# One Trainium2 core, sparse attention into a softplus MLP: weight loads gated by real waits, grouped reads of PSUM banks, query copies on GpSimd

## The chip, the cores and the metric

The kernel runs on one core of one Trainium2 chip. The metric is device time in microseconds (us). Engines are called PE (TensorE, matmuls), PEld (its weight loads), DVE (VectorE), ACT (ScalarE), POOL (GpSimd) and SP (SyncE, which here only issues DMAs). A change of under about 1% cannot be told from none.

## The reference

Inputs are fp32: q, k and v of 4 batches x 8 heads x 768 positions x 64, w_in of 512 x 2048 and w_out of 2048 x 512. The keys are cut into 24 chunks of 32. For each query an upper bound of its product with each chunk is taken from the chunk's smallest and largest key values; only the 6 best causal chunks are attended.

```python
k_min = np.min(k_chunks, axis=3);  k_max = np.max(k_chunks, axis=3)
ub = sum(maximum(q * k_min, q * k_max), axis=-1)        # per query and chunk, causal only
top_chunks = np.argsort(ub, axis=-1)[..., -top_k:]       # top_k = 6
scores = where(chosen chunk and causal, q @ k.T / sqrt(64), -1e9)
x = (softmax(scores) @ v)  laid out as (3072 tokens, 512)
h = x @ w_in;  g = maximum(h, 0) + log1p(exp(-abs(h)));  out = g @ w_out
```

## The kernel before

The work is cut into 12 blocks of 256 query rows (4 batches x 3 blocks). A block n has these steps, named as the code names its tasks: loads of k, q and v (`ld`), transposes of k and q, chunk minima and maxima `kx` from the transposed keys, copies `ka` and `kb` of the keys (head 0 and head 1 of a pair), the positive and negative part of the queries `qp` and `qn`, the bound matmuls `ub`, top-6 selection (`uba`, `max`, `lt`), a mask that is transposed (`mT`) and put into the query tiles as extra contraction rows (`ma`, `mb`), the second query tile `qa`, then per head pair p the score matmuls `s` with `exp` on ACT (`ex`), the diagonal mask on POOL (`cm`), `av`, normalisation (`rc`, `nm`), and the transposed result x (`oT`, `xe`). The MLP of a block is 16 tasks `h` (4 matmuls of 256 columns each), `exp` and `ln(1+.)` on ACT, and 16 tasks `y` (2 matmuls of 512 columns each). The first three blocks, the ramp, are loaded as fp32 and transposed by PE (L398, L459); from block 3 on POOL casts to bf16 (`ck`, `cq`, `cv`; L365, L367) and SP issues DMA transposes (L419, L469, L559, L659).

The order on each engine is set by a planner in the kernel: every task has a duration, a priority and its dependencies, and a discrete-event loop (`Graph.schedule`) lays the tasks out; they are then emitted in that order. Nothing else keeps the order: each engine works through its own list, and waits only for semaphores that the data or a reused buffer need. All loads of blocks go through the SP queue (a few through ACT's), the two weight loads through POOL's queue, in four pieces each (L326, L334). Where two engines read one PSUM bank, the second waits for the first.

In the planner `gates` makes block 2's loads follow the third piece of w_in, and `LGATE` makes the loads of block 3 and later follow the third piece of w_out. These are dependencies of the plan alone: the instructions have no wait for them.

Of the kernel before, what the change touches and what calls it, by code (L numbers as in the profile page):

```python
# [20 lines left out]
NP = H // 2  # L21
QB = 256
# [11 lines left out]
LEAD = 30  # L34
DMA_START = 1.3
MSTART = 20.0
AHEAD = 1.16
ORDER = ("0", "1", "wi", "2", "wo")
# [16 lines left out]
class Graph:  # L55
# [34 lines left out]
    def schedule(self):  # L90
# [58 lines left out]
        while True:  # L149
# [24 lines left out]
            for e in LAT:  # L174
# [14 lines left out]
                for b in t.bufs:  # L189
                    if b.slot is None:  # L190
# [16 lines left out]
def build(nc, tiles):  # L207
# [67 lines left out]
    for i in range(2):  # L275
        add("DVE", 0.3, lambda i=i: DV.memset(T("bd", i), 0.0), -9 + i * 30, w=[("bd", i)], name="bd0")
        add("DVE", 1.1, lambda i=i: DV.memset(T("mr", i), 0.0), -8 + i * 12, w=[("mr0", i)], name="mr0")
        add("DVE", 0.1, lambda i=i: DV.memset(T("v", i)[:, :, :, D:D + 1], 1.0), -8 + i * 30,
            w=[("v1", i)], name="v1")
        add("DVE", 1.35, lambda i=i: DV.memset(T("kb", i)[0:32], 0.0), -7 + i * 30, w=[("kb0", i)], name="kb0")  # L280

        def oh(which, i, blk):
            ks = slice(blk * QB, (blk + 1) * QB)
            dst = T("ka", i)[64:96, :, ks] if which == "ka" else T("kb", i)[32:64, :, ks]
            PO.tensor_copy(dst, T("ohb")[:, ks].unsqueeze(1).to_broadcast([32, NP, QB]))
        for blk in range(NBLK):
            for which in ("ka", "kb"):
                add("POOL", 0.95, lambda which=which, i=i, blk=blk: oh(which, i, blk), -6 + i * 34 + blk * 5, r=["ohb"],
                    w=[(which + "c", i, blk)], name="oh" + which)
# [49 lines left out]
    def gates(n):  # L339
        return [landed["wi", 2]] if n == 2 else []  # L340

    ramp_loads(0, -100)
    ramp_loads(1, -90)
    w_in_load(-50, [landed[1, "q", 1]])
    ramp_loads(2, -80)
    w_out_load(-40, [landed[2, "q", 1]])
    LGATE = [landed["wo", 2]]
# [26 lines left out]
    def prep(n):  # L374
# [12 lines left out]
        if ramp:  # L387
            for hh in range(2):
# [19 lines left out]
                for m in range(2):  # L408
                    add("DVE", 0.6, lambda m=m, red=red: red(m), pr + 0.1, r=[kT], w=[(kx, m, hh)], name=f"kx{n}")
                add("ACT", 0.48, lambda kab=kab: kab("ka", slice(0, 64)), pr + 0.2, r=[kT],  # L410
                    w=[("ka", i, j, hh) for j in js], name=f"ka{n}")
                add("ACT", 0.48, lambda kab=kab: kab("kb", slice(64, 128)), pr + 0.2, r=[kT],
                    w=[("kb", i, j, hh) for j in js], name=f"kb{n}")
# [59 lines left out]
        for hs in ([[0], [1]] if ramp else [[0, 1]]):  # L473
# [7 lines left out]
            add("DVE", 0.09 + 0.13 * len(hs), lambda sl=sl: DV.tensor_copy(T(qa)[0:64, sl], T(qb)[0:64, sl]), pr + 2,  # L481
                r=[(qb, hh, z) for hh in hs for z in range(3)], w=[(qa, hh, 0) for hh in hs], name=f"qa{n}")
        bds = [("bdw", i, h, k_) for h in range(2) for k_ in range(blk + 1)]
        ubp = ps("o")
        ns = len(sel)
        halves = [[0], [1]]
        for hs in halves:
# [15 lines left out]
            def uba(es=es, ne=ne):  # L503
# [239 lines left out]
def kernel(  # L743
# [30 lines left out]
    one("ohb", "ohb", [32, S], BF16)  # L774
    one("cmask", "cmask", [128, NQT, NCH], F32)
# [44 lines left out]
```

## Time and profile before

| what | value |
|---|---|
| median of 3 runs | 281.82 us (281.0 to 283.47) |
| the profiled execution's own time | 280.93 us |
| its span, first to last instruction | 279.2 us |
| busy PE / ACT / DVE / POOL | 248.9 / 198.6 / 152.5 / 98.3 us |
| HBM read / written | 27.26 / 6.29 MB |
| chain that ended last, by engine | PE 62%, DVE 16%, DMA 13%, ACT 4% |

PE is busy for 89% of the span, and the idle rest is not spread evenly: most of it lies in the first 53 us. Busy shares are means over stages, so the stages have to be read one by one. Times of rows are from the span's start.

### The profile page before, as it was taken

To read this page: it belongs to the slowest core of one execution; us is meant where nothing else is said; L and a number is where in the kernel's file an instruction comes from. 1 tells how busy PE (TensorE), PEld (TensorE's weight loads), DVE (VectorE), ACT (ScalarE), POOL (GpSimd) and SP (SyncE) were. 2 spreads that over 40 slices of the span, in tenths; PEclk is the share of its full clock that TensorE was granted. 3 is DMA by queue.
4 is the path that set the end of the run, shared out by engine and by line. 5 is a ranking of instruction groups with operands and counts; after the bars stand their busy time and mean duration, and the time that the engine had idled before them with its cause. 6 is when DMAs were issued, how large, how long until landed. Compare 5 with 4: busy or idle time off the path is not lost.

```text
span 279.2 us, 6479 instructions
## 1 busy us (share of the span) xinstructions
PE 248.9 (89%) x2424; PEld 184.4 (66%) x2460; DVE 152.5 (55%) x558; ACT 198.6 (71%) x355; POOL 98.3 (35%) x188
## 2 busy tenths in 40 slices
PE   3356796999999899989899988999999999999994
PEld 2244584777767668767676855866767777677661
DVE  6787837823979978479669536536326211020001
ACT  2436278898649876999796975686958969949470
POOL 8958327036318453438344432021311201100000
PEclk9999589999999999999999999999999999999999
DMA  8999979949999999999999993412312211040101
GB/s 165 218 182 164 197 135 184 189 80 134 241 231 191 258 220 198 248 187 173 248 218 222 215 230 82 113 41 59 94 39 73 44 39 40 1 77 38 40 38 75
DMA packets 120800, 39.23 MB, mean 140 GB/s; under 512 B 113600, under 2 KB 117696, under 8 KB 120768
## 3 DMA queue, kind: packets, MB, share of 16 engines
q1 hardware_dynamic: 113392, 33.83, 62.7%
q0 software_dynamic: 4224, 4.19, 9.3%
q10 hardware_dynamic: 3152, 0.79, 1.6%
q8 instruction: 19, 0.31, 0.5%
q14 instruction: 13, 0.11, 0.1%
HBM read 27.26 MB, written 6.29 MB: 120 GB/s over the span
## 4 chain that ended last, share of the span: by engine, by line
PE 62%; DVE 16%; DMA 13%; ACT 4%; issue 3%; SPq 1%; POOL 0%; DVEq 0%; ACTq 0%
PE ps L679 22%; PE ps L700 21%; PE ps L597 10%; DMA kt<-kq 6%; PE ps L622 5%; DMA xf<-in_q_dram 4%; DVE kx L423 3%; DVE kx L405 2%; DMA qab<-kq 2%; ACT pt L606 2%; DVE qpn L479 1%; DMA xf<-in_k_dram 1%; ACT kb L402 1%; DVE qpn L477 1%; DVE oall L643 1%
## 5 line engine op out<-in xcount | busy, mean ns | idle before, releaser
L679 PE MATMUL ps<-x,w_in_sb 128*128 128x256 bf16 x768 | 106.5, 273 | 1.6 <-DVE kx L405 1.4
L606 ACT ACTIVATE pt<-ps 128x512 bf16<-128x512 f32 (+1 forms) x192 | 93.1, 568 | 16.8 <-PE ps L597 14.7
L700 PE MATMUL ps<-w_out_sb,g 128*128 128x512 bf16 x348 | 99.4, 379 | 1.3
L679 PEld LDWEIGHTS <-w_in_sb 128*128 128x128 bf16 x768 | 72.8, 98 | 25.1 <-issue 1.7
L685 ACT ACTIVATE e<-ps 128x512 f32<-128x512 f32 x96 | 57.1, 612 | 39.9 <-PE ps L679 39.5
L612 POOL TENSOR_SCALAR_AFFINE_SELECT pt<-pt 128x256 bf16<-128x256 bf16 x96 | 40.2, 429 | 102.8 <-ACT pt L606 102.8
L689 ACT ACTIVATE g<-e 128x1024 bf16<-128x1024 f32 x48 | 51.6, 1075 | 0.8
L700 PEld LDWEIGHTS <-g 128*128 128x128 bf16 x384 | 35.1, 98 | 13.1
L705 DVE COPY yo<-ps 128x512 f32<-128x512 f32 x24 | 16.4, 685 | 45.7 <-PE ps L700 45.7
L367 POOL CAST kq<-xf 128x512 bf16<-128x512 f32 x36 | 22.5, 627 | 35.2 <-DMA xf<-in_k_dram 22.4
L631 DVE RECIPROCAL st<-ps 128x4 f32<-128x4 f32 x48 | 8.4, 176 | 45.3 <-PE ps L622 37.6
L597 PE MATMUL ps<-qab,kb 128*128 128x256 bf16 x192 | 32.9, 269 | 0.2
L622 PEld LDWEIGHTS <-pt 128*128 128x128 bf16 x672 | 27.5, 99 | 7.6 <-POOL pt L612 2.2
L597 PE MATMUL ps<-qab,ka 96*128 96x256 bf16 x192 | 30.1, 269 | 1.8 <-DVE qab L551 1.0
L622 PE MATMUL ps<-v,pt 128*128 128x65 bf16 x672 | 29.8, 196 | 2.0 <-POOL pt L612 1.9
L423 DVE TENSOR_REDUCE kx<-kt 128x32 bf16<-128x1024 bf16 x18 | 21.2, 1208 | 7.8 <-DMA kt<-kq 7.8
L597 PEld LDWEIGHTS <-ka 96*128 96x128 bf16 x192 | 18.4, 101 | 10.6 <-issue 2.4
L597 PEld LDWEIGHTS <-kb 128*128 128x128 bf16 x192 | 17.6, 102 | 6.7 <-DVE qab L551 0.2
L643 DVE TENSOR_TENSOR oall<-ps,st 128x256 bf16<-128x256 f32 x36 | 15.1, 420 | 0.8
L514 DVE MAX8 ub<-ub 128x8 f32<-128x24 f32 (+2 forms) x160 | 14.1, 160 | 0.1
L498 PE MATMUL ps<-bd,qpn 128*128 128x32 bf16 (+2 forms) x80 | 7.2, 179 | 7.7 <-DVE qpn L477 4.7
L365 POOL CAST v<-xf 128x512 bf16<-128x512 f32 x18 | 11.1, 621 | 6.8 <-DMA xf<-in_v_dram 6.7
(56 smaller groups left out, 179.3 us busy)
## 6 DMA issues: line engine op xcount, KB each, us to landing
out_dram<-yo SPq DMA_DIRECT2D x24, 256.0 KB, 2.9
xf<-in_v_dram SPq DMA_DIRECT2D x23, 256.0 KB, 4.6
xf<-in_k_dram SPq DMA_DIRECT2D x18, 256.0 KB, 4.0
xf<-in_q_dram SPq DMA_DIRECT2D x18, 256.0 KB, 4.9
w_in_sb<-in_moe_w_in_dram POOLq DMA_DIRECT2D x4, 512.0 KB, 11.0
w_out_sb<-in_moe_w_out_dram POOLq DMA_DIRECT2D x4, 512.0 KB, 11.1
xf<-in_k_dram SPq DMA_DIRECT2D x10, 128.0 KB, 4.2
xf<-in_q_dram SPq DMA_DIRECT2D x10, 128.0 KB, 3.9
```

The lines of the kernel that those rows point to most:

```text
L367: PO.tensor_copy(T(b_)[:, :, t], T(xf).rearrange("s (p c) -> s p c", p=NP))
L423: DV.tensor_reduce(T(kx)[:, m].rearrange("d p (t c) -> d p t c", t=NT), T(kt).rearrange("d (p t) (c s) -> d p t c s", t=NT, s=CH), axis=AX ...
L597: PE.matmul(T(sp)[:, z * QB:z * QB + QB - q0], kk[r0:r1, p, (j + z) * 128:(j + z + 1) * 128], qq[r0:r1, p, q0:QB], start=True, stop=True)
L606: AC.activation(T(pt)[:, j:j + 2].rearrange("k j c -> k (j c)")[:, 0:w], T(sp)[:, 0:w], ACT.Exp, scale=SCALE)
L612: PO.affine_select(out=diag, in_=diag, compare_op=ALU.is_ge, fill=0.0, base=0, channel_multiplier=-1, pattern=[[0, 2], [1, 128]])
L622: PE.matmul(o[:, u, h], T(pts[h])[:, j, c0:c0 + 128], T("v", i)[:, j, 2 * p + h, :], start=(j == 0), stop=(j == t0 + u))
L643: DV.tensor_tensor(dst, o[:, :, :, 0:D], T(st).to_broadcast([128, NT, 2, D]), op=ALU.mult)
L679: PE.matmul(o, T("w_in")[:, dt, ft * 128:(ft + 1) * 128], T(x)[:, dt], start=(dt == 0), stop=(dt == KDM - 1))
L685: AC.activation(T(e)[:, f2 * 2:f2 * 2 + 2].rearrange("f a s -> f (a s)"), T(hp), ACT.Exp)
L689: AC.activation(T(gb)[:, f4 * 4:(f4 + 1) * 4], T(e), ACT.Ln, bias=1.0)
L700: PE.matmul(T(y), T(gb)[:, f, u * 128:(u + 1) * 128], T("w_out")[:, f, :], start=(f == 0), stop=(f == KFF - 1))
L705: add("DVE", 0.6, lambda y=y, yo=yo: DV.tensor_copy(T(yo), T(y)), pr, r=[y], w=[yo], name=f"yo{n}")
```

## The change

Five edits. (1) Load order: block 2 is loaded straight behind blocks 0 and 1; the first weight piece is issued after a one-element POOL copy that reads the last query tile of block 2 (`hold_pool`), so that POOL waits until it has landed; w_out follows behind a second such copy; block 3's loads on SP stand behind two tiny DMAs that read the third piece of w_in and of w_out (`hold_sp`). (2) One engine at a time on a PSUM bank in the plan (`held`), and the pairs of reads are grouped: `kx` does minimum and maximum in one task, `ka` and `kb` are one task; the bound matmuls use a bank per half. (3) The ramp's `qa` copies go from DVE to POOL. (4) The constant work for the second set of key and value buffers (three DVE memsets and six POOL copies `oh`) moves behind the landing of w_in's last piece and gets a later priority. (5) Planned durations are adjusted.

```diff
-ORDER = ("0", "1", "wi", "2", "wo")
+ORDER = ("b0", "b1", "b2", "wi", "wo")
+GATEQ = {"w_in": 2, "w_out": 2}
...
         def fits(t):
             for b in t.bufs:
+                if any(k for x, k in b.held.items() if x != t.eng):
+                    return False
...
+    def background(i, pr, after):
+        add("DVE", 0.2, lambda: DV.memset(T("bd", i), 0.0), pr, w=[("bd", i)], name="bd0", after=after)
+        add("DVE", 0.1, lambda: DV.memset(T("v", i)[:, :, :, D:D + 1], 1.0), pr, w=[("v1", i)], name="v1", after=after)
+        add("DVE", 1.35, lambda: DV.memset(T("kb", i)[0:32], 0.0), pr, w=[("kb0", i)], name="kb0", after=after)
         for blk in range(NBLK):
             for which in ("ka", "kb"):
+                add("POOL", 1.04, lambda which=which, blk=blk: oh(which, i, blk), pr + blk, r=["ohb"],
+                    w=[(which + "c", i, blk)], name="oh" + which, after=after)
...
+    def hold_pool(key, pr):
+        b_ = XF[key]
+        return [add("POOL", 0.1, lambda: PO.tensor_copy(T("scratch")[0:1, 0:1], T(b_)[0:1, 0:1]), pr, r=[b_], w=["scratch"],
+                    name="hold")]
+    def hold_sp(nm, c4, pr):
+        def fn():
+            src = T("w_in")[0:1, 0, c4 * 512:c4 * 512 + 2] if nm == "w_in" else T("w_out")[0:1, c4 * 4, 0:2]
+            SP.dma_start(out=T("scratch2")[0:1, 0:2], in_=src)
+        return [add("SP", 0.6, fn, pr, r=[(nm, c4)], w=["scratch2"], name="hold")]
...
+            (w_in_load if nm == "w_in" else w_out_load)(-100 + k_ * 10, hold_pool(("q", last, 1), -100 + k_ * 10))
+            gate = hold_sp(nm, GATEQ[nm], -91 + k_ * 10)
+    LGATE = gate
...
-                for m in range(2):
-                    add("DVE", 0.6, lambda m=m, red=red: red(m), pr + 0.1, r=[kT], w=[(kx, m, hh)], name=f"kx{n}")
...
+                add("DVE", 1.3, lambda red=red: (red(0), red(1)), pr + 0.1, r=[kT], w=[(kx, m, hh) for m in range(2)],
+                    name=f"kx{n}")
+                add("ACT", 1.06, lambda kab=kab: (kab("ka", slice(0, 64)), kab("kb", slice(64, 128))), pr + 0.2, r=[kT],
+                    w=[(w_, i, j, hh) for w_ in ("ka", "kb") for j in js], name=f"ka{n}")
...
+            qe_, qd = ("POOL", 0.6) if ramp else ("DVE", 0.35)
+            add(qe_, qd, lambda sl=sl: (PO if ramp else DV).tensor_copy(T(qa)[0:64, sl], T(qb)[0:64, sl]), pr + 1.8,
                 r=[(qb, hh, z) for hh in hs for z in range(3)], w=[(qa, hh, 0) for hh in hs], name=f"qa{n}")
...
-        ubp = ps("o")
...
+            ubp = ps("o")
...
+    background(1, BG, [landed["wi", 3]])
```

How the order moves is seen best in two places. First DVE in block 0, from the first chunk maxima to the first bounds. Before, `kb_76` and `v_74` are the second buffer set, L477 and L479 are `qp` and `qn`, L481 is `qa`, L505 is `uba`:

```order
L405 TENSOR_REDUCE kx_102<-ps_139 128x16 [waits Activation_49] x2
L278 MEMSET v_74 128x48
L280 MEMSET kb_76 32x1536
L440 COPY bd_73<-kx_102 64x8x8 [waits DVE_49]
L477 TENSOR_SCALAR qpn_98<-qab_93 128x2x128 [waits Activation_49]
L479 TENSOR_SCALAR qpn_99<-qab_93 128x2x128
L481 COPY qab_92<-qab_93 64x512 x2
L505 TENSOR_TENSOR ub_104<-ps_142,cmask 128x4x8 [waits PE_49,Pool_49]
```

The same place with the change:

```order
L432 TENSOR_REDUCE kx_104<-ps_141 128x16 [waits PE_49,Activation_49]
L432 TENSOR_REDUCE kx_104<-ps_141 128x16
L465 COPY bd_75<-kx_104 64x8x8 [waits DVE_49]
L502 TENSOR_SCALAR qpn_100<-qab_95 128x2x128 [waits Activation_49]
L504 TENSOR_SCALAR qpn_101<-qab_95 128x2x128
L531 TENSOR_TENSOR ub_106<-ps_144,cmask 128x4x8 [waits PE_49,Pool_49]
L540 MAX ub_106<-ub_106 128x8 [waits DVE_49]
```

The two memsets and the two copies are gone from between, and both reductions of a bank stand together. Second POOL around the weight loads. Before, w_in is issued behind the first diagonal mask of block 0 (L612), which follows casts of v (L569) and the `oh` copies (L285):

```order
L569 CAST v_70<-xf_82 128x8x64 [waits DMAHW1_49]
L285 COPY kb_76<-ohb 32x4x256 [waits Pool_49]
L285 COPY ka_75<-ohb 32x4x256
L285 COPY kb_76<-ohb 32x4x256
L612 AFFINE_SELECT pt_110<-pt_110 128x2x128 [waits Activation_49,Pool_49]
L326 DMA w_in_sb<-in_moe_w_in_dram 128x4x512 x4
L612 AFFINE_SELECT pt_111<-pt_111 128x2x128 [waits Activation_49]
```

The same place with the change (L638 is the mask, L507 a `qa` copy, L354 the hold):

```order
L638 AFFINE_SELECT pt_113<-pt_113 128x2x128 [waits Activation_49]
L507 COPY qab_97<-qab_96 64x512
L595 CAST v_72<-xf_82 128x8x64 [waits DMAHW6_49,DMAHW3_49,DMAHW0_49]
L354 CAST scratch<-xf_87 1x1 [waits DMAHW2_49]
L338 DMA w_in_sb<-in_moe_w_in_dram 128x4x512 x4
L354 CAST scratch<-xf_87 1x1 [waits Pool_49]
L638 AFFINE_SELECT pt_114<-pt_114 128x2x128 [waits Activation_49]
L346 DMA w_out_sb<-in_moe_w_out_dram 128x4x512 x4
L638 AFFINE_SELECT pt_116<-pt_116 128x2x128 [waits Activation_49]
```

w_in now stands behind all eight masks of block 0, and w_out behind the first mask of block 1 (before, behind the seventh). On SP the two hold DMAs stand between block 2's last load and block 3's first.

## Rows read from the trace of the kernel before

**Rows 1.** By stage: stretch, length, busy PE, PEld, DVE, ACT, POOL, clock, DMA, GB/s.

```profile
0.00:35.40 35.40, 19.24 (x131) 13.96 (x132) 27.79 (x96) 13.72 (x27) 25.74 (x42) 0.88 1.12 185
35.40:53.40 18.00, 15.10 (x185) 12.80 (x184) 12.01 (x51) 14.02 (x28) 6.71 (x13) 0.95 0.94 165
53.40:69.00 15.60, 15.39 (x186) 11.76 (x189) 4.81 (x14) 14.68 (x30) 7.20 (x15) 1.00 0.81 126
131.00:174.00 43.00, 38.80 (x383) 28.64 (x388) 27.55 (x83) 32.73 (x58) 16.77 (x33) 1.00 1.00 200
174.00:279.20 105.20, 100.55 (x910) 72.31 (x925) 29.25 (x119) 73.72 (x126) 11.43 (x28) 1.00 0.20 54
```

**Rows 2.** The chain that ended last, 125 to 180 us: start, us, what.

```profile
141.04 4.68 DMA kt<-kq
```

**Rows 3.** PE in order of time: start, us, instructions [idle before].

```profile
18.60 0.80 PE L597 MATMUL ps<-qab,ka 96*128 96x256 bf16 x4 [0.56 <-DVE qab L551]
19.51 1.06 PE L398 MATMUL ps<-identf,xf 128*128 128x128 f32 x4
...
32.46 0.91 PE L597 MATMUL ps<-qab,ka 96*128 96x256 bf16 x4 [0.41 <-DVE qab L551]
...
35.40 1.06 PE L679 MATMUL ps<-x,w_in_sb 128*128 128x256 bf16 x4
...
68.22 0.83 PE L622 MATMUL ps<-v,pt 128*128 128x65 bf16 x22
```

**Rows 4.** ACT in order of time, block 0.

```profile
7.03 0.58 ACT L402 CAST kb<-ps 64x512 bf16<-64x512 f32 x1 [0.76 <-DVE kx L405]
...
9.57 1.07 ACT L463 CAST qab<-ps 128x512 bf16<-128x512 f32 x2
```

**Rows 5.** DVE in order of time, blocks 0 and 1.

```profile
10.72 1.34 DVE L280 MEMSET kb<- 32x1536 uint32 x1 [0.23 <-issue]
...
14.65 1.32 DVE L481 COPY qab<-qab 64x512 bf16<-64x512 bf16 x2
...
24.30 0.35 DVE L477 TENSOR_SCALAR qpn<-qab 128x512 bf16<-128x512 bf16 x1 [0.93 <-ACT qab L463]
...
28.15 0.16 DVE L525 CAST mr<-ub 128x4 bf16<-128x4 f32 x1
...
28.36 1.01 DVE L525 CAST mr<-ub 128x4 bf16<-128x4 f32 x1
```

**Rows 6.** One source line, 0 to 60 us: ns min/median/max, first to last start.

```profile
L481 DVE COPY qab<-qab x6: 274/379/1121, 14.6 to 48.8; 64x512 bf16<-64x512 bf16 x6
```

**Rows 7.** The chain that ended last, 61 to 78 us: paces of PE at full speed.

```profile
61.12 0.66 PE ps L622 x22
61.78 0.60 PE ps L597 x6
62.38 0.44 PE ps L679 x4
...
77.63 1.73 PE ps L700 x8
```

**Rows 8.** POOL in order of time (POOL DMA rows are issues).

```profile
4.77 1.03 POOL L285 COPY ka<-ohb 32x1024 bf16<-32x1024 bf16 x1
...
20.26 3.11 POOL L326 DMA_DIRECT2D w_in_sb<-in_moe_w_in_dram  x4
...
28.23 1.11 POOL L285 COPY ka<-ohb 32x1024 bf16<-32x1024 bf16 x1
...
65.21 0.41 POOL L612 TENSOR_SCALAR_AFFINE_SELECT pt<-pt 128x256 bf16<-128x256 bf16 x1 [0.40 <-ACT pt L606]
...
67.29 0.41 POOL L612 TENSOR_SCALAR_AFFINE_SELECT pt<-pt 128x256 bf16<-128x256 bf16 x1 [0.55 <-ACT pt L606]
```

**Rows 9.** SP's queue: start, us, issue of block 3's transpose.

```profile
63.10 1.33 SPq L419 DMA_TRANSPOSE kt<-kq  x1
```

**Rows 10.** Tile w_out_sb, 0 to 110 us: its four pieces, issue to landing.

```profile
DMA to landing us min/median/max: 7.3/11.1/14.2
```

More of the change, by code (lines that the diff above doesn't have):

```diff
@@ L34 @@
 LEAD = 30
+BG = 40
 DMA_START = 1.3
@@ L47, in __init__ @@
         self.pool, self.kind, self.left, self.slot = pool, kind, 0, None
+        self.held = {}
 class Task:
@@ L114, in done @@
                 b.left -= 1
+                if b.pool == "ps":
+                    b.held[t.eng] -= 1
                 if b.left == 0:
@@ L189, in schedule @@
                 for b in t.bufs:
+                    if b.pool == "ps":
+                        b.held[t.eng] = b.held.get(t.eng, 0) + 1
                     if b.slot is None:
@@ L274, in build, with oh @@
     add("POOL", 0.45, c_ident, -7, w=["ident"], name="ident")
[L275 to L285, printed above, removed]
+    def oh(which, i, blk):
+        ks = slice(blk * QB, (blk + 1) * QB)
+        dst = T("ka", i)[64:96, :, ks] if which == "ka" else T("kb", i)[32:64, :, ks]
+        PO.tensor_copy(dst, T("ohb")[:, ks].unsqueeze(1).to_broadcast([32, NP, QB]))
+    def background(i, pr, after):
+        add("DVE", 0.2, lambda: DV.memset(T("bd", i), 0.0), pr, w=[("bd", i)], name="bd0", after=after)
+        add("DVE", 0.1, lambda: DV.memset(T("v", i)[:, :, :, D:D + 1], 1.0), pr, w=[("v1", i)], name="v1", after=after)
+        add("DVE", 1.35, lambda: DV.memset(T("kb", i)[0:32], 0.0), pr, w=[("kb0", i)], name="kb0", after=after)
         for blk in range(NBLK):
             for which in ("ka", "kb"):
-                add("POOL", 0.95, lambda which=which, i=i, blk=blk: oh(which, i, blk), -6 + i * 34 + blk * 5, r=["ohb"],
-                    w=[(which + "c", i, blk)], name="oh" + which)
+                add("POOL", 1.04, lambda which=which, blk=blk: oh(which, i, blk), pr + blk, r=["ohb"],
+                    w=[(which + "c", i, blk)], name="oh" + which, after=after)
+    for i in range(2):
+        add("DVE", 0.5, lambda i=i: DV.memset(T("mr", i), 0.0), -8, w=[("mr0", i)], name="mr0")
+    background(0, -6, ())
     srcs = T("src") if nc else None
@@ L304, in build, with ramp_loads @@
     landed = {}
-    def ramp_loads(n, base):
+    def ramp_loads(n, base, gate):
         for nm in "kqv":
@@ L319, in ld @@
                             q_.dma_start(out=dst[:, u * 4:u * 4 + 4], in_=rows(nm, n, u)[:, t * 4:t * 4 + 4])
-                landed[n, nm, t] = add(eng, 0.6 if nm == "v" else 1.2, ld, base + "kqv".index(nm), w=[b_], dma=1.17, lat=0.5, name=f"ld{nm}{n}{t}", after=gates(n))
+                landed[n, nm, t] = add(eng, 0.6 if nm == "v" else 1.2, ld, base + "kqv".index(nm), w=[b_], dma=1.17,
+                                       lat=0.5, name=f"ld{nm}{n}{t}", after=gate)
     def w_in_load(base, after):
@@ L337, in w_out_load @@
                                    name="ldw_out", after=after)
[L339 to L347, printed above, removed]
+    def hold_pool(key, pr):
[7 more added lines that the diff above has]
+        return [add("SP", 0.6, fn, pr, r=[(nm, c4)], w=["scratch2"], name="hold")]
+    gate, last = (), None
+    for k_, what in enumerate(ORDER):
+        if what[0] == "b":
+            n = int(what[1])
+            ramp_loads(n, -100 + k_ * 10, gate)
+            last = n
+            gate = ()
+        else:
+            nm = "w_in" if what == "wi" else "w_out"
+            (w_in_load if nm == "w_in" else w_out_load)(-100 + k_ * 10, hold_pool(("q", last, 1), -100 + k_ * 10))
+            gate = hold_sp(nm, GATEQ[nm], -91 + k_ * 10)
+    LGATE = gate
     def loads(n):
@@ L407, in red @@
                                      op=ALU.max if m == 0 else ALU.min)
-                for m in range(2):
-                    add("DVE", 0.6, lambda m=m, red=red: red(m), pr + 0.1, r=[kT], w=[(kx, m, hh)], name=f"kx{n}")
[L410 to L413, printed above, removed]
+                add("DVE", 1.3, lambda red=red: (red(0), red(1)), pr + 0.1, r=[kT], w=[(kx, m, hh) for m in range(2)],
+                    name=f"kx{n}")
+                add("ACT", 1.06, lambda kab=kab: (kab("ka", slice(0, 64)), kab("kb", slice(64, 128))), pr + 0.2, r=[kT],
+                    w=[(w_, i, j, hh) for w_ in ("ka", "kb") for j in js], name=f"ka{n}")
         else:
@@ L480, in prep @@
                 pr + 1.3, r=rq, w=[(qn, hh) for hh in hs], name=f"qn{n}")
-            add("DVE", 0.09 + 0.13 * len(hs), lambda sl=sl: DV.tensor_copy(T(qa)[0:64, sl], T(qb)[0:64, sl]), pr + 2,
+            qe_, qd = ("POOL", 0.6) if ramp else ("DVE", 0.35)
+            add(qe_, qd, lambda sl=sl: (PO if ramp else DV).tensor_copy(T(qa)[0:64, sl], T(qb)[0:64, sl]), pr + 1.8,
                 r=[(qb, hh, z) for hh in hs for z in range(3)], w=[(qa, hh, 0) for hh in hs], name=f"qa{n}")
         bds = [("bdw", i, h, k_) for h in range(2) for k_ in range(blk + 1)]
-        ubp = ps("o")
         ns = len(sel)
@@ L491, in prep, with ubm @@
             psl = slice(pp[0], pp[-1] + 1)
-            def ubm(pp=pp):
+            ubp = ps("o")
+            def ubm(pp=pp, ubp=ubp):
                 o = T(ubp)[:, 0:NT * H * ncc].rearrange("s (t p h c) -> s t p h c", t=NT, p=NP, h=2)
@@ L501, in prep, with uba @@
                 w=[(ubp, hh) for hh in hs], name=f"ub{n}")
-            def uba(es=es, ne=ne):
+            def uba(es=es, ne=ne, ubp=ubp):
                 o = T(ubp)[:, 0:NT * H * ncc].rearrange("s (t e c) -> s t e c", t=NT, c=ncc)
@@ L774 @@
     one("ohb", "ohb", [32, S], BF16)
+    one("scratch", "scratch", [1, 8], BF16)
+    one("scratch2", "scratch2", [1, 8], BF16)
     one("cmask", "cmask", [128, NQT, NCH], F32)
```

## Prediction

> **What bounds the kernel now.** I read the busy time by stage first, then the chain of waits, then the single engines in order of time. The stages [rows 1] show where PE is idle: 35.4 - 19.2 = 16.2 us before the first MLP matmul, 2.9 us from there to 53.4, 0.2 us to 69, 4.2 us between 131 and 174, and 4.6 us in the last 105 us. After 53 us PE is the bound, but for one stretch: between 131 and 174 us the chain runs through loads and DMA transposes such as the one of 4.68 us [rows 2], with the DMA engines busy all the time [rows 1]. So there are two clocks to watch. One is how much PE work is done by a given time; the other is when the stream of block loads from block 3 on gets going. Its first visible step is SP's first DMA transpose at 63.10 [rows 9]. What the change does before 53 us is worth only what both let through.
>
> The ramp itself is a chain of short DVE, ACT and PE steps: DVE is busy 27.8 of the first 35.4 us, ACT only 13.7 [rows 1]. First scores of block 0 come at 18.60, of block 1 at 32.46, the first MLP matmul at 35.40, and the last `av` of block 2 ends at 68.22 + 0.66 = 68.9 [rows 3, 7].
>
> **The change part by part.** *Block 0.* The memset of the second key buffer, 1.34 us with 0.23 idle before it [rows 5], leaves the path, and a 0.1 us one with it: -1.7. ACT's key copies waited 0.76 us for a DVE reduction of the same bank [rows 4], and DVE waited as long for ACT. Grouped in pairs, the two engines work on different banks; of the four reductions' 4 us I take 1.0 off, with 0.2 as the low bound, because the query copies at 9.57 are not much earlier (their own transposes wait for q), and 1.5 as the high one, two such waits. The two `qa` copies go to POOL, -1.3 [rows 5]; POOL does them behind six `oh` copies that end near 11.2 (4.77 and six at 1.03 to 1.08 apiece) [rows 8], so they are ready before the mask is. Against that, PE's transposes of block 1 now stand between the two mask transposes: +1.06 [rows 3]. Sum -2.9: first scores near 15.7.
>
> *Block 1.* On one bank DVE's pair of reductions now goes ahead of ACT's pair of copies, which gives 1.3 us back to the path of the query copies; part of that was waited for before. I move the first `qp`, 24.30 before [rows 5], to 22.4. From there to the first scores it took 8.16 us. Off this go two `qa` copies at the median 0.38 [rows 6] = 0.8, the 0.85 us that a cast of four columns lost at 28.36 (1.01 us against 0.16 just before it) beside a POOL copy that the change moves away [rows 5, 8], and about 1.2 us of second-half selection that now stands behind the first half's mask. Left 5.3: first scores of block 1 near 27.7, 4.8 us earlier.
>
> *Block 2 and the first MLP work.* In the new order its key transposes, reductions and query copies stand ahead of or among the scores of block 1, and the first bound matmul of block 2 comes before the first `h`. Behind the first scores DVE has two reduction pairs (2.7), two mask copies (0.8), `nm`, `xe`, `bd`, `qp` and `qn` (about 2.1): 6 us at least, so the first `h` starts near 34.2, only 1.2 us earlier. But what PE still has to do up to the last `av` of block 2 is less. Counted from the new order and priced by the paces at full speed [rows 7]: 18 `h` at 0.44 = 7.9, 9 `y` pairs at 0.43 = 3.9, 24 score tiles at 0.20 = 4.8 and three of block 1 at 0.6, four `av` at 0.66 and four of block 1 at 0.42 (14 matmuls for 22) = 4.3, small transposes 1.4: 22.9 us. ACT's list from the first scores of block 1 to that point is some 27 us, so it ends no later. For waits between the three engines I add 2 us (before, 2.9 were idle in the 18 us stage and 0.2 in the next). The last `av` then ends near 59.1, 9.8 us earlier. By that point 2 `h` and 4 `y` fewer have been done than before, 2.6 us of work. **PE term: -7.2.**
>
> *The weights.* w_in's issue, 20.26 before [rows 8], moves behind the eight masks of block 0, a cast and the landing of q of block 2: near 25.5. Its pieces need 7.3 us for the first, if they land as w_out's did [rows 10], so 32.8: 1.4 us ahead of the first `h`, and the next pieces follow by some 2.7 us (0.52 MB at 190 GB/s [rows 1]) where `h` needs one in 3.5 or more. w_out follows at once; 4.2 MB of both need 22 us from 27, so its third piece is there near 46 to 48, and `y` begins near 46. This cover is thin: without it PE, which works in order, waits.
>
> *The hold DMAs.* Each is one tiny transfer on SP behind which block 3's six loads stand. These loads now start near 48 instead of during w_in and w_out, and land by 55. That is still before they are used: POOL casts them behind the seventh and eighth mask of block 2, and those come with its last scores. Before, the eighth mask was 68.9 - 67.29 = 1.6 us ahead of the last `av` [rows 8]. So 59.1 - 1.6 + 0.4 + 0.6 = 58.5 for the second cast, and SP's transpose then instead of at 63.10 [rows 9]. **Stream term: -4.6.** Nobody else waits behind the holds on SP; behind those on POOL stand the masks of block 1, which come later anyway.
>
> *Background on POOL.* Six `oh` copies, 6.2 us [rows 8], move among the masks of block 2. Each can hold a mask by up to 1.03 us, and `av` with it; the stage has PE work to fill in, so I cost it at nothing, at most 2.
>
> *Sum.* PE reaches equal work 7.2 us earlier, the load stream starts 4.6 us earlier. Since DMA sets the pace between 131 and 174, I take the smaller one and next to nothing of the rest: **-4.8 us**. The profiled execution took 280.93 us, 0.9 below the median; it would become 276.1, and the median 281.82 becomes **277.0**. Bounds: 274.5 if the PE term passes whole, 279.3 if the ramp terms are worth half.
>
> POOL and DVE get in each other's way in this trace: the cast at 28.36 ends at 29.37, just after POOL's copy from 28.23 to 29.34 [rows 5, 8], and one DVE `qa` copy takes between 0.27 and 1.12 us [rows 6]. The Trainium skill (SBUF — State Buffer, section "Who interferes with whom") says that DVE copies and tensor-scalar work in the two-port mode and GpSimd share one pair of ports, and that the one that comes second is blocked for the whole instruction; the trace agrees with its 1.01 us. That speaks against `qa` on POOL, and gives the third rival.
>
> **The rivals.** *The stream is not earlier (17%).* The load stream alone decides, and the masks of block 2 are held by the `oh` copies and by ACT, so that the second cast comes near 62 to 63 as before. For it: the whole 131 to 174 stage hangs on DMA. Against it: ACT gets its work 5 us earlier. Time 281.
>
> *PE's term passes whole (12%).* The 4.2 us of idle PE between 131 and 174 shrink, since PE has other work there; for it, PE is 90% busy even in that stage. With 7.2 us or a little more: 274.
>
> *POOL copies block DVE (9%).* Each `qa` copy on POOL lasts about 0.52 us (half of the 1.03 us of twice its columns) and stops a DVE instruction on the path for that long; four stand in blocks 0 and 1, so 2.1 us come back: 279.1.
>
> *Slower: the weights come too late (7%).* One mechanism: w_in's issue stands behind the last mask of block 0 in POOL's order, and through w_out also holds block 3's loads on SP. Block 3's loads have some 3.5 us of cover before the cast and the stream 4.6 us of gain; from 8 us late on, the end moves us by us. At 12 us late (issue at 37, which needs block 0's last scores to come later than block 1's do before) it is 4 us slower: 286.
>
> **How the numbers follow.** Forecast 55%, the rivals 17, 12, 9 and 7%. The likeliest's own range is 274.5 to 279.3; the 80% range reaches to the first and second rival: 272 to 281.5. A measurement here tells about 1% from no change, that is under 279.0 and over 284.6. Faster: 52 of the forecast's 55, the 12, and 4 of the port rival's 9: 68%. Same: 25%. Slower: 7%.
>
> **What would show it.** Right: block 0's first scores near 15.7, block 1's near 27.7, first `h` near 34 with no wait for w_in, the last `av` of block 2 near 59, SP's first transpose near 58.5, and about as much PE idle after 90 us as before. Wrong: a PE wait on the w_in tile; first transpose on SP later than 62; PE idle growing between 90 and 180 by what the ramp gained; the ACT key copies still waiting 0.7 us for DVE.

## The result and the profile after

The changed kernel takes 272.8 us (median of 4, 272.12 to 273.36); the kernel before, timed beside it, 281.89 us (4 runs). The ratio is 0.967, 95% interval 0.962 to 0.972: faster by 3.3%. Forecast were 277.0 us and a range of 272 to 281.5, so the sign holds, the range holds by 0.8 us, and the size does not: 9.1 us gained at the medians against 4.8. The profiled executions took 280.93 and 273.36 us, 7.6 apart, with spans of 279.2 and 271.7; the other 1.5 us is that the profiled execution of before lies 1.0 under its median and that of after 0.6 over. Shares below are of the 7.5 us between the spans.

The windows of the changed kernel, in the stages and columns of [rows 1] (the clock is the TensorE clock that was granted, as a share of full speed):

```profile
0.00:35.40 35.40, 22.38 (x168) 16.88 (x169) 28.55 (x97) 19.98 (x39) 27.14 (x51) 0.94 1.00 176
35.40:53.40 18.00, 17.01 (x228) 14.12 (x228) 12.03 (x52) 14.29 (x28) 10.49 (x16) 0.93 1.16 200
53.40:69.00 15.60, 15.44 (x150) 11.22 (x151) 7.98 (x19) 11.80 (x21) 6.99 (x13) 1.00 0.80 165
131.00:174.00 43.00, 40.41 (x412) 30.27 (x416) 27.81 (x94) 33.69 (x62) 16.46 (x32) 1.00 1.10 195
174.00:271.70 97.70, 92.77 (x829) 65.82 (x840) 25.20 (x97) 68.76 (x117) 10.70 (x26) 0.99 0.18 50
```

PE idles 13.0 us in the first stage instead of 16.2, and 1.0 instead of 2.9 in the second. PE in order of time, at the events that the prediction named:

```profile
15.80 0.53 PE L623 MATMUL ps<-qab,ka 96*128 96x256 bf16 x2
...
27.86 0.76 PE L623 MATMUL ps<-qab,ka 96*128 96x256 bf16 x6 [0.58 <-DVE qab L577]
...
35.12 1.03 PE L705 MATMUL ps<-x,w_in_sb 128*128 128x256 bf16 x4
...
59.30 0.60 PE L705 MATMUL ps<-x,w_in_sb 128*128 128x256 bf16 x4
...
60.17 0.84 PE L648 MATMUL ps<-v,pt 128*128 128x65 bf16 x22
60.84 1.46 PE L726 MATMUL ps<-w_out_sb,g 128*128 128x512 bf16 x6
```

First scores of block 0 at 15.80 (18.60 in [rows 3]; 15.7 forecast), of block 1 at 27.86 (32.46; 27.7), the first MLP matmul at 35.12 (35.40; 34.2), the last `av` of block 2 ends at 60.84, where the next `y` begins (68.9; 59.1). The first MLP matmul follows without a wait, for w_in or for anything else.

ACT in order of time, the key copies of block 0, which answer to [rows 4]:

```profile
5.85 0.58 ACT L429 CAST ka<-ps 64x512 bf16<-64x512 f32 x1 [3.76 <-PE ps L425]
6.44 0.58 ACT L429 CAST kb<-ps 64x512 bf16<-64x512 f32 x1
7.04 0.58 ACT L429 CAST ka<-ps 64x512 bf16<-64x512 f32 x1
7.63 0.58 ACT L429 CAST kb<-ps 64x512 bf16<-64x512 f32 x1
```

They run back to back; the wait of 0.76 us for DVE is gone. POOL around the weight loads, answering to [rows 8]:

```profile
25.18 0.61 POOL L595 CAST v<-xf 128x512 bf16<-128x512 f32 x1
25.73 0.18 POOL L354 CAST scratch<-xf 1x1 bf16<-1x1 f32 x1
25.86 3.12 POOL L338 DMA_DIRECT2D w_in_sb<-in_moe_w_in_dram  x4
```

The hold at 25.73 waits for nothing that the trace shows: the query tile that it reads has landed. SP's queue, answering to [rows 9]:

```profile
36.66 0.75 SPq L360 DMA_DIRECT2D scratch<-w_in_sb  x1
47.67 0.56 SPq L360 DMA_DIRECT2D scratch<-w_out_sb  x1
48.34 1.00 SPq L387 DMA_DIRECT2D xf<-in_k_dram  x2
...
59.80 1.39 SPq L444 DMA_TRANSPOSE kt<-kq  x1
```

The holds here do wait (15.2 us for w_in's third piece, 6.3 us for w_out's), and block 3's loads leave at 48.34. Its first key transpose is at 59.80: 3.3 us earlier than in [rows 9], 1.3 later than forecast.

### The profile page after: what moved, and what is told of

Same layout as the page of the kernel before. It is cut to its first block, busy times and chain, and to the rows that moved or that the text cites. A ratio compares the mean times of both kernels' runs of the same rounds, so it can differ in the third digit from the quotient of the medians.

```text
span 271.7 us, 6500 instructions
## 1 busy us (share of the span) xinstructions
PE 248.0 (91%) x2424; PEld 183.6 (68%) x2460; DVE 151.8 (56%) x552; ACT 199.2 (73%) x355; POOL 102.1 (38%) x196
## 3 DMA queue, kind: packets, MB, share of 16 engines
q1 hardware_dynamic: 113400, 33.83, 65.1%
## 4 chain that ended last, share of the span: by engine, by line
PE 69%; DVE 15%; DMA 10%; issue 3%; ACT 1%; SPq 1%; DVEq 0%; ACTq 0%
PE ps L705 26%; PE ps L726 23%; PE ps L623 9%; PE ps L648 6%; DMA kt<-kq 4%; DVE kx L432 2%; DMA qab<-kq 2%; DMA xf<-in_v_dram 2%; PE ps L425 2%; DMA xf<-in_q_dram 1%; DVE ub L540 1%; DMA xf<-in_k_dram 1%; DVE qab L577 1%; DVE bd L465 1%; DVE qpn L504 1%
## 5 line engine op out<-in xcount | busy, mean ns | idle before, releaser
L638 POOL TENSOR_SCALAR_AFFINE_SELECT pt<-pt 128x256 bf16<-128x256 bf16 x96 | 39.7, 422 | 92.2 <-ACT pt L632 91.8
L394 POOL CAST kq<-xf 128x512 bf16<-128x512 f32 x36 | 23.4, 654 | 34.2 <-DMA xf<-in_k_dram 23.8
L623 PE MATMUL ps<-qab,kb 128*128 128x256 bf16 x192 | 31.8, 264 | 0.9 <-DVE ub L531 0.7
L623 PEld LDWEIGHTS <-ka 96*128 96x128 bf16 x192 | 17.9, 100 | 9.3 <-issue 1.5
L540 DVE MAX8 ub<-ub 128x8 f32<-128x24 f32 (+2 forms) x160 | 14.3, 162 | 0.2
L429 ACT CAST ka<-ps 64x512 bf16<-64x512 f32 x6 | 3.5, 578 | 12.3 <-PE ps L425 10.7
## 6 DMA issues: line engine op xcount, KB each, us to landing
w_out_sb<-in_moe_w_out_dram POOLq DMA_DIRECT2D x4, 512.0 KB, 15.5
```

Of the source, the lines that this page charges most:

```text
L394: PO.tensor_copy(T(b_)[:, :, t], T(xf).rearrange("s (p c) -> s p c", p=NP))
L540: DV.max(out=T(ub_sb)[:, t, e, NCH:NCH + 8], in_=T(ub_sb)[:, t, e, 0:ncc])
L623: PE.matmul(T(sp)[:, z * QB:z * QB + QB - q0], kk[r0:r1, p, (j + z) * 128:(j + z + 1) * 128], qq[r0:r1, p, q0:QB], start=True, stop=True)
L638: PO.affine_select(out=diag, in_=diag, compare_op=ALU.is_ge, fill=0.0, base=0, channel_multiplier=-1, pattern=[[0, 2], [1, 128]])
```

## The experiments

All runs in one table. Idle is a stretch's length less PE's busy time in it, from the windows of the profiled execution; "first" and "last" are SP's first and last key transpose (blocks 3 and 11). Two executions of the same kernel (before and its control c0, after and its control c1) differ by up to 1.6 us in an idle cell, by 1.7 in "last" and by 2.0 in the span, so single cells carry that much doubt.

| kernel | median us | ratio to before, 95% | span | idle 0 to 60 | 60 to 131 | 131 to 174 | 174 to end | first | last |
|---|---|---|---|---|---|---|---|---|---|
| before | 281.89 | | 279.2 | 19.2 | 2.3 | 4.2 | 4.7 | 63.10 | 165.51 |
| c0, before again | 282.21 | 1.000 (0.997 to 1.004) | 280.1 | 20.1 | 3.2 | 2.6 | 5.6 | 63.87 | 166.18 |
| after | 272.8 | 0.967 (0.962 to 0.972) | 271.7 | 14.1 | 2.1 | 2.6 | 4.9 | 59.80 | 159.63 |
| c1, after again | 273.2 | 0.965 (0.960 to 0.970) | 273.7 | 15.3 | 2.3 | 2.9 | 4.1 | 59.88 | 161.34 |
| e1, no holds | 274.38 | 0.971 (0.968 to 0.975) | 272.9 | 14.1 | 3.3 | 2.7 | 3.7 | 58.38 | 160.99 |
| e2, `qa` on DVE | 273.2 | 0.967 (0.963 to 0.971) | 272.9 | 13.4 | 3.7 | 2.2 | 4.1 | 57.87 | 160.92 |
| e3, background early | 274.69 | 0.973 (0.969 to 0.977) | 273.6 | 15.5 | 2.3 | 2.9 | 4.1 | 59.80 | 161.28 |
| e4, stream late | 279.11 | 0.991 (0.987 to 0.995) | 277.1 | 14.5 | 5.2 | 2.5 | 3.7 | 64.97 | 165.35 |
| d1, all but the load order | 279.18 | 0.986 (0.982 to 0.991) | 277.4 | 17.9 | 2.9 | 2.5 | 3.7 | 62.99 | 166.43 |
| d2, the load order alone | 276.8 | 0.978 (0.973 to 0.983) | 275.3 | 17.8 | 3.2 | 1.6 | 4.2 | 60.07 | 163.12 |
| d3, d2 without holds | 277.2 | 0.980 (0.975 to 0.985) | 275.2 | 16.3 | 3.3 | 1.6 | 5.5 | 59.78 | 162.23 |
| s1, casts early, with a slip | 275.36 | 0.972 (0.968 to 0.977) | 274.8 | 14.5 | 3.9 | 2.4 | 4.1 | 59.75 | 163.32 |
| s2, casts early | 274.16 | 0.970 (0.964 to 0.975) | 273.5 | 15.5 | 4.2 | 3.1 | 4.8 | 54.65 | 161.33 |
| v, no v loads | 270.09 | 0.956 (0.951 to 0.960) | 268.6 | 14.3 | 2.4 | 0.7 | 4.8 | 58.41 | 155.82 |

**Which part of the change does it.** *d1* goes back to the old load order, without holds; the plan is made anew.

```diff
-ORDER = ("b0", "b1", "b2", "wi", "wo")
+ORDER = ("b0", "b1", "wi", "b2", "wo")
...
-        t.fn()
+        if t.name != "hold":
+            t.fn()
```

> All of the change but its load order: block 2 planned behind w_in as before, no holds issued, and the planner lays the rest out anew. Theory R (shorter chains in the ramp make the gain): most of it stays, -6 to -9 us against before, 273 to 276; block 2's keys come later, so the last av of block 2 comes some 2 us later than in the changed kernel. Theory O (loading block 2 ahead of the weights makes the gain): -1 to -3 us, 279 or more.

*d2* is the kernel before with the new load order and its holds, and nothing else of the change.

```diff
-ORDER = ("0", "1", "wi", "2", "wo")
+ORDER = ("b0", "b1", "b2", "wi", "wo")
+GATEQ = {"w_in": 2, "w_out": 2}
```

> The kernel before with the load order and its real waits alone. Theory R: DVE and ACT have the same chains in blocks 0 and 1, so first scores of block 0 still near 18.6 and of block 1 near 32; within 2 us of before, 280 to 284. Theory O: most of the gain, 276 or less.

Everything but the load order gives 1.4%, the load order alone 2.2%. The product of the two ratios, 0.964, is what the whole change does (0.967 and 0.965), so the two parts add up. Both runs lie between what the two theories expected (4.1 and 6.5 us gained on the kernel before, timed beside them at 283.29): neither part is the whole gain. That the shorter chains of blocks 0 and 1 would be the whole cause fell with d2: there the first scores come at 19.57 and 33.83, later than before, and about two thirds of the gain is there.

*c1* is the changed kernel once more, timed beside d1 and d2.

> The changed kernel as it is, once more, so that the variants are compared with it on one chip. Every theory: a ratio of 0.967 to the kernel before, within 0.005.

Its ratio repeats that of the first timing, so the 3.3% stand.

**Is it the real waits?** *e1* keeps the changed kernel's order and leaves out the hold instructions (the last three lines of d1's diff). *d3* does the same to d2.

> The changed kernel in its own order, with the two one-element POOL copies and the two tiny SP transfers left out, so that nothing holds the load order but the queues. Theory R (the gain comes from shorter chains on DVE, ACT and POOL in the ramp): POOL's hold waited for nothing (it ran at 25.73, right behind a cast that ended at 25.79), so only SP's holds matter; block 3's loads then run from about 22 us beside w_in, whose pieces come up to 6 us later, and the first h (35.1) waits for up to 4 us. Expected 272.8 + 0 to + 3, and SP's first block 3 transpose still at 59 to 62, since POOL's masks set it. Theory O (the real waits are the gain): most of the 9 us is lost, 278 or more.

> The kernel before, planned with the changed load order and its holds, as in the run that had the load order alone (276.8 us), but the hold instructions are not issued: the order is the same, no instruction waits for a weight. Theory L (the order that the planner makes from the new loads counts): within 1.5 us of 276.8, ratio to before 0.973 to 0.983. Rival W (the real waits count, because they keep transfers from colliding): most of the gain goes, 280 us or more, ratio over 0.988, and block 2's or block 3's data land later than in the run with the holds.

d3 is 0.4 us from d2, inside the 1.5 that was set as the limit, so what counts in the load order is the plan. Block 3's loads leave at 24.85 in d3 and at 51.30 in d2, and the end does not notice. e1 is 1.2 to 1.6 us slower than the changed kernel's two medians, with overlapping intervals against both: if the waits bring anything there, it is under 1%. The wait of the first `h` that was feared in e1 did not come (the first `h` is at 34.99, without one), and SP's first transpose comes at 58.38, ahead of the 59 to 62 expected. What the plan does differently is seen in PE's transposes of block 2's keys. Before:

```profile
39.91 0.61 PE L398 MATMUL ps<-identf,xf 128*128 128x128 f32 x4
...
43.31 1.03 PE L679 MATMUL ps<-x,w_in_sb 128*128 128x256 bf16 x8 [0.55 <-DVE kx L405]
45.62 0.60 PE L679 MATMUL ps<-x,w_in_sb 128*128 128x256 bf16 x4 [0.84 <-DVE kx L405]
47.10 0.20 PE L498 MATMUL ps<-bd,qpn 128*128 128x48 bf16 x1 [0.21 <-DVE qpn L477]
```

and in d3, where no wait was added:

```profile
24.78 0.63 PE L413 MATMUL ps<-identf,xf 128*128 128x128 f32 x4
27.12 0.63 PE L413 MATMUL ps<-identf,xf 128*128 128x128 f32 x4
```

A plan that loads block 2 ahead of the weights prepares it 15 us earlier, in a stretch in which PE has idle time; PE's waits for block 2's `kx` and `qp` on DVE, in the rows of before, are gone. So is most of the idle time of the second stage, 2.9 us in [rows 1]. The window of that stage in d3:

```profile
35.40:53.40 18.00, 17.55 (x224) 14.52 (x223) 11.00 (x54) 16.54 (x34) 5.22 (x12) 0.94 1.23 200
```

PE idles 0.45 us there in d3 and 0.4 in d2. In d1, with the old load order, it idles 3.7 us there, but 14.3 instead of 16.2 before 35.4. So the shorter chains are seen in the first stage and the load order in the second. This is not all that the load order does: between 1.4 and 3.7 us of the 3.9 to 4.9 between the spans lie ahead of 60 us in d2 and d3, by which profile of before is taken, and where the rest comes from is not shown.

**The chains of blocks 0 and 1.** *e2* puts the `qa` copies back on DVE, at the same places of the order.

```diff
-            add(qe_, qd, lambda sl=sl: (PO if ramp else DV).tensor_copy(T(qa)[0:64, sl], T(qb)[0:64, sl]), pr + 1.8,
+            add(qe_, qd, lambda sl=sl: DV.tensor_copy(T(qa)[0:64, sl], T(qb)[0:64, sl]), pr + 1.8,
```

> The changed kernel in its own order, with the ramp's six query copies issued on DVE at the same places. If a copy on POOL takes the work off DVE's path: the six cost 0.38 us each on DVE, four of them ahead of the first scores of blocks 0 and 1, so +1 to +2 us: 274 to 275. If a copy on POOL blocks DVE for as long as it saves (the queries' positive part took 0.64 to 0.75 us beside POOL copies in the changed kernel's trace, 0.29 alone): within 0.5 us of 272.8, or faster.

The first scores come at 15.04 instead of 15.80, the last `av` of block 2 starts at 58.23 instead of 60.17 and the first key transpose at 57.87 instead of 59.80, and the time is the same. PE's idle time to 60 us is 0.7 less than in the profile of after (1.9 less than in its control), and between 60 and 131 it is 1.6 more (1.4): here a gain of the ramp was lost again behind it.

*e3* issues the second buffer set's memsets behind block 0's `kx`, and its `oh` copies behind block 0's casts of v.

```diff
+        if t.name in left:
+            left[t.name] -= 1
+            if left[t.name] == 0:
+                for u in back["DVE" if t.name == "kx0" else "POOL"]:
+                    u.fn()
```

> The changed kernel in its own order, but the second buffer set's three DVE memsets stand behind block 0's reductions again and its six POOL copies behind block 0's two casts. Theory R: the memsets cost 1.7 us on the path to block 0's first scores (15.80 becomes about 17.5) and the six copies 6.4 us on POOL from 13.6 to 20, so that the first masks of block 0 wait 2.5 us and some DVE instructions run into them. Each us of the ramp comes out at the end: +2 to +3.5 us, 275 to 276. If what follows absorbs it: under +0.7.

First scores come at 17.42 (+1.6), near the 1.7 that the prediction took for the memsets, and the first MLP matmul at 36.41 (+1.3). The memsets alone do not make this: the first `uba` is 1.1 us later (14.67 against 13.59), and behind it two steps of the selection (L548) take 0.50 and 0.69 us beside the `oh` copies, 0.19 each in the changed kernel. The median is 1.5 to 1.9 us up on the changed kernel's two, a little under the 2 to 3.5 expected, but the interval of its ratio overlaps those of after and its control.

**The load stream.** *e4* delays it: six tiny transfers on SP, each waiting for the one before, stand ahead of block 3's first transpose.

```diff
+                if n == NRAMP:
+                    for z in range(6):
+                        SP.dma_start(out=T("scratch2")[0:1, 2:4], in_=T("w_in")[0:1, 0, 2 * z:2 * z + 2])
```

> The changed kernel with six tiny transfers on SP ahead of block 3's first transpose (59.80), 0.55 us of issue each at the least and more where one waits for the last: the whole stream of transposes and loads behind it starts 3.3 us later or more, while PE's ramp is untouched. Theory S of the prediction (DMA sets the pace of the middle, the stream's start is what counts): the end moves by as much as the stream, +3 us or more, 276. Theory P (PE's work is the bound and the stream has slack): under +1 us, 273 to 274.

SP's queue, PE's wait and PE's window (columns as in [rows 1]) in e4:

```profile
54.39 10.49 SPq L446 DMA_DIRECT2D scratch<-w_in_sb  x6
64.97 1.33 SPq L447 DMA_TRANSPOSE kt<-kq  x1
```

```profile
73.01 0.20 PE L527 MATMUL ps<-bd,qpn 128*128 128x16 bf16 x1 [3.85 <-DVE qpn L505]
```

```profile
70.00:80.00 10.00, 6.99 (x32) 3.53 (x33) 4.82 (x24) 1.65 (x2) 3.79 (x6) 0.66 1.25 243
```

The transpose is 5.2 us later, the span 5.4 us longer (3.4 against the control) and the median 5.9 to 6.3. PE runs dry at 69.2 us, waits 3.85 us for block 3's `qp`, and then works at the lower clock for a while (0.66 granted on average from 70 to 80). So late data do cost, about one for one.

*s1* was to start the stream earlier, by moving block 3's key casts ahead of block 2's last masks.

```diff
+    move(("ck3",), "ldk3", -1)
+    move(("cq3",), "cm2", 6)
```

> The changed kernel in its own order, but on POOL block 3's two key casts stand behind the sixth mask of block 2 instead of behind the seventh and the eighth, and its two query casts behind the seventh. Block 3's keys land near 53 to 54, so SP's first transpose should go from 59.8 to about 55.5 and the next loads with it. Theory S (the stream of transposes and loads sets the end: in the runs so far the end lies 112 us behind the last transpose): the end comes 2.5 to 4.5 us earlier, 268 to 270. Theory P (PE has no idle time to give): within 1 us of the changed kernel. Third: the stream starts earlier but ends no earlier, because it is paced inside by DMA or by SP's waits for PE: within 1 us too, with the last transpose at 159 to 161.

It did not test that: the move put one query cast of block 3 ahead of the load that it should follow (that half of the queries is then the older one), and the load waited for the cast. SP's queue in s1:

```profile
50.34 7.13 SPq L387 DMA_DIRECT2D xf<-in_q_dram  x2
...
59.75 2.36 SPq L444 DMA_TRANSPOSE kt<-kq  x1
```

The two query loads take 7.13 us of SP instead of 2.72, and the first transpose stays at 59.75. It took 275.36 us (ratio 0.972, 0.968 to 0.977). *s2* does it properly.

```diff
+    move(("ck3",), "ldk3")
+    move(("cq3",), "ldq3")
```

> The changed kernel, with the key casts of block 3 on POOL moved right behind the last of their loads in program order (ahead of the last masks of block 2), and its query casts likewise; nothing else moves. Only block 3's first transpose on SP should come earlier, from about 59.8 to about 55.5 us. Theory S (the start of the block stream sets the end, one for one): the end comes 2.5 to 4.5 us earlier, 268 to 270.5 us, 112 us behind the last key transpose as in all runs so far. Rival P (the stream is paced inside: by the buffers that a block must free, by SP's in-order waits, by the work that PE still has to do): blocks 4 and 5 are back at the old times, and the end is within 1 us of the changed kernel's, 272 to 274.

SP's key transposes of blocks 3 to 6, and POOL on the way there, in s2:

```profile
54.65 1.97 SPq L444 DMA_TRANSPOSE kt<-kq  x1
...
65.06 2.58 SPq L444 DMA_TRANSPOSE kt<-kq  x1
...
78.21 2.30 SPq L444 DMA_TRANSPOSE kt<-kq  x1
...
95.23 1.49 SPq L444 DMA_TRANSPOSE kt<-kq  x1
```

```profile
81.34 1.70 POOL L638 TENSOR_SCALAR_AFFINE_SELECT pt<-pt 128x256 bf16<-128x256 bf16 x4 [2.41 <-ACT pt L632]
...
92.15 0.55 POOL L638 TENSOR_SCALAR_AFFINE_SELECT pt<-pt 128x256 bf16<-128x256 bf16 x1 [4.77 <-ACT pt L632]
```

The same places in the changed kernel (block 3's is at 59.80):

```profile
68.00 2.55 SPq L444 DMA_TRANSPOSE kt<-kq  x1
...
81.37 2.61 SPq L444 DMA_TRANSPOSE kt<-kq  x1
...
95.38 1.37 SPq L444 DMA_TRANSPOSE kt<-kq  x1
```

```profile
82.34 1.17 POOL L638 TENSOR_SCALAR_AFFINE_SELECT pt<-pt 128x256 bf16<-128x256 bf16 x3 [0.32 <-ACT pt L632]
...
93.18 0.55 POOL L638 TENSOR_SCALAR_AFFINE_SELECT pt<-pt 128x256 bf16<-128x256 bf16 x1 [4.77 <-ACT pt L632]
```

5.2 us of lead at block 3 are 2.9 at block 4, 3.2 at block 5 and 0.15 at block 6, and the end is no earlier. The stream is held from inside: POOL, in order, has the next casts behind masks, and these wait for ACT's exponentials of scores that PE comes to in its own order. At the mask at 81.34 POOL waits 2.41 us instead of 0.32, and of its lead 1.0 us is left; the next long wait is 4.77 us in both. PE is busy 14.88 of the 15 us from 60 to 75 in both kernels, so it has no idle time there in which to come to them sooner. Theory S fell. Rival P holds for the end, though blocks 4 and 5 are not back at the old times, as it expected; that is block 6. In all runs the end lies 111 to 114 us behind the last key transpose, and that does not make the stream the cause: both hang on PE's order.

*c0* is the kernel before again.

> The kernel before once more, as its own control: its profiled execution (280.93 us) was the shortest of its runs. Ratio 1.000 within 0.4%; a profiled execution of 281 to 283 us, block 3's first transpose near 63, the last key transpose between 165 and 168, and the end 112 to 114 us behind it. If the end does not lie that far behind the last transpose, the rule read from the other runs does not hold for the kernel before.

Its first transpose is at 63.87 and its last at 166.18, 113.9 us ahead of the end, as expected. Its 2.6 us of idle PE between 131 and 174, against 4.2 in the first profile, show how little a single profile says of that stage.

*v* leaves out the loads of v from block 4 on, about a third of the bytes that the stream loads; the v tiles keep older values, so the output is not the reference's.

```diff
+                    if nm == "v" and n > NRAMP:
+                        return
```

> The changed kernel without the loads of v from block 4 on (the v tiles keep older values, so the output is not the reference's): about a third of the bytes that the block loads move goes, while every transpose, cast, mask and matmul stays. Theory D (the DMA engines pace the stream between block 3 and block 11): the stream from first to last key transpose, 100 us, gets shorter by 3 us or more, and the end comes earlier by as much, 267 to 270 us. Rival Q (the stream is paced by what its steps wait for on POOL, SP and PE, not by transfers): stream and end stay within 1 us of the changed kernel's.

The windows in v, columns as in [rows 1]:

```profile
131.00:174.00 43.00, 42.26 (x449) 32.17 (x454) 30.35 (x96) 35.92 (x66) 17.67 (x33) 1.00 0.71 148
```

The time falls by 2.7 to 3.1 us against the changed kernel and its control. The stream is 97.4 us long, 2.4 less than in after and 4.1 less than in the control: at the edge of what theory D asked for, and outside rival Q. PE idles 0.7 us in this stage instead of 2.6 and 2.9. So the loads of v are worth about 2 us of PE's waiting there. Whether by their bytes or by their turns in SP's queue is not told apart: without them the share of the DMA engines falls from 1.10 to 0.71, and SP's rows in the stretch add up to 22.0 us instead of 33.4.

## Why the prediction was right in sign and short in size

**Right at the first scores, in block 0 with luck.** -2.8 and -4.6 us, -2.9 and -4.8 forecast. The pieces of block 0 stand in DVE's rows. Before ([rows 5] has L481):

```profile
9.58 0.69 DVE L405 TENSOR_REDUCE kx<-ps 128x16 bf16<-128x512 f32 x1 [0.65 <-ACT kb L402]
...
11.99 0.51 DVE L440 COPY bd<-kx 64x64 bf16<-64x64 bf16 x2
...
15.89 0.27 DVE L505 TENSOR_TENSOR ub<-ps,cmask 128x32 f32<-128x32 f32 x2
```

and after (L465 and L502 are shown further down):

```profile
7.05 2.48 DVE L432 TENSOR_REDUCE kx<-ps 128x16 bf16<-128x512 f32 x4 [1.72 <-ACT kb L429]
...
13.59 0.18 DVE L531 TENSOR_TENSOR ub<-ps,cmask 128x32 f32<-128x32 f32 x1
...
15.10 0.60 DVE L577 COPY qab<-ps 32x256 bf16<-32x256 bf16 x2
```

Three terms are near their price: the reductions end 0.7 us earlier (10.27 to 9.53; 1.0 forecast), the memsets' 1.7 us behind them are gone (as forecast), and so are the 1.2 us of the `qa` copies (1.3). But from the first `bd` copy to the first `uba`, `qa` left out, it takes 4.0 us (9.57 to 13.59) instead of 2.7 (11.99 to 14.65): +1.4 that is in no term of the sum, beside POOL's copies (below). And from the first `uba` to the scores it takes 2.2 us instead of 2.7, -0.5 where the sum had +1.06 for PE's transposes: these stand where it put them, but DVE's mask copies, for which the scores wait as well, end only at 15.70, 0.1 us ahead of the scores, so they cost no more than that. The two misses cancel, and that is luck. In block 1 the first `qp` comes 1.4 us earlier (22.89; 1.9 forecast), and the way from there to the scores is 3.2 us shorter (2.9).

**Too large: the PE term.** -7.2 was forecast. The last `av` of block 2 came 8.1 us earlier; less the 2.6 us of work not done (2.9 by PE's busy time up to there, 49.62 and 46.72 us), that is -5.5, and PE's idle time to 60 us fell by 5.05. Two pieces of the sum were short. The first MLP matmul came 0.9 us later than forecast. And the work from there to the last `av` was priced at 22.9 us at full speed; between 35.4 and 53.4 us the granted clock was 0.93, and rows such as the 1.03 us for four matmuls at 35.12, which take 0.60 later, show the lower level. With the lower level at 0.50, as granted in e4 from 74 to 78 us, 0.93 means some 2.5 of the 18 us at half speed, 1.3 us of lost work (an estimate from these rows). The 2 us added for waits were more than was needed (1.1 us idle from 35.4 to 60).

**Too large: the stream term.** -4.6 forecast, -3.3 measured; it follows the last masks, the eighth of which comes at 58.81, 1.3 us later than forecast, as the last `av` is 1.7 late.

**The step that failed** is the one that put the two together: "Since DMA sets the pace between 131 and 174, I take the smaller one and next to nothing of the rest". By it the 7.5 us between the spans could not have been more than 3.3. The spans make a plain account: PE's busy time changes by -0.9 us, its idle time by -6.6, of which -5.05 lie before 60 us, -0.2 from 60 to 131, -1.6 from 131 to 174, and +0.3 after. The control pair gives -6.9 in all and -4.7 before 60 us. What the ramp gained was kept, and the stage that was to swallow it did not grow: it shows 2.6 to 2.9 us of idle after, 4.2 and 2.6 before. Cut at 90 us the two pairs of profiles agree better: between 60 and 90 PE idles 1.3 and 0.8 us more than before, and from 90 us on, where the prediction expected as much idle time as before, 2.9 and 3.0 us less (8.05 in both, from 10.95 and 11.06). Which of the edits takes those 3 us away is not shown. The chain of waits names DMA in that stage [rows 2], and DMA has its cost there, as v shows; but PE was busy 38.8 of its 43 us [rows 1], and the blocks' transfers move with PE's order, because POOL comes to their casts only as PE gets on with the scores. s2 shows the other side: the stream's start, for which the smaller term stood, has no worth of its own once it is early enough; e4 shows that it has little to spare, for of 5.2 us of delay PE waited 3.85. -5.05 in the ramp, -1.6 in later waits (-2.2 by the controls), -0.9 of busy time (which the controls do not confirm: +0.5), and 1.5 from the two profiles' places in their runs make 9.0 of the 9.1.

**The rivals.** "PE's term passes whole" came nearest to the mechanism: priced at 274 with a PE term that was 2 us too large, and given 12%. That 274 lies near the 272.8 is partly luck: the 2 us too many stand in for the later waits. "The stream is not earlier" is out by 59.80. The weights were not late: w_in's first piece landed 5.5 us after its issue at 25.86, 3.8 us ahead of its use.

**POOL copies and DVE.** The block is real, a price at the end is not seen. DVE in block 0 of the changed kernel, and POOL beside it:

```profile
9.57 1.65 DVE L465 COPY bd<-kx 64x64 bf16<-64x64 bf16 x2
11.25 0.75 DVE L502 TENSOR_SCALAR qpn<-qab 128x256 bf16<-128x256 bf16 x1
...
20.31 0.17 DVE L465 COPY bd<-kx 64x64 bf16<-64x64 bf16 x1
```

```profile
9.08 1.03 POOL L287 COPY ka<-ohb 32x1024 bf16<-32x1024 bf16 x1
10.15 1.03 POOL L287 COPY kb<-ohb 32x1024 bf16<-32x1024 bf16 x1
11.25 1.22 POOL L507 COPY qab<-qab 64x512 bf16<-64x512 bf16 x2
```

A copy of 64 columns takes 0.17 us by itself, and a pair of them 1.65 us beside POOL's copies, ending as POOL's does. The rule cited in the prediction (the Trainium skill, SBUF — State Buffer, "Who interferes with whom": the one that comes second is blocked for the whole instruction) agrees. A `qa` copy on POOL takes 0.60 to 0.73 us, not the 0.52 of the prediction. With `qa` on DVE, e2's first scores come 0.8 us sooner in block 0, where that rival had 1.04 (two copies), and the end does not move.

## What to carry to other kernels

When a gain early in a kernel meets a later stage whose chain runs through another resource, do not take the smaller of two terms: take the idle time of the bounding engine, stretch by stretch, and ask whether it can grow where the gain is supposed to be lost. An event on the way (a last `av`, a first transpose) that comes earlier is worth nothing by itself, as e1, e2 and s2 show, and not even less idle time up to then, for in e2 it came back by 131 us: the bounding engine's idle time over the whole span is what counts. And where a planner sets the order, a changed dependency works through the order it makes: look for what it moves into idle time before crediting the wait.

## What was not expected of the hardware

- A late stream is paid twice: by the wait, and by the clock behind it. Against the changed kernel, e4 has 2.2 us more of idle time and 3.2 us more of busy time (251.2 against 248.0; against the control 1.4 and 2.0), with the granted clock at 0.66 from 70 to 80 us, after PE had idled 3.85 us.
- Six tiny transfers in a chain, each waiting for the one before, take 10.49 us on SP: 1.75 us each, in the trace of e4.
- Transfers that compete for a while need not show at the end when they have cover: with block 3's six loads among the weight pieces (d3), w_in's pieces take 11.0 us to land at the median, and 8.2 with the loads held back by 26 us (d2); the times are 0.4 us apart.
